# Recurrent attention issued between the MLP matmuls of earlier tokens, with its state kept in PSUM

## The chip, the cores and the metric

The kernel runs on one core of one Trainium2 chip. The metric is the time of one execution on the device in microseconds (us); the median of several executions is quoted. The span of a profile is a little shorter, since it runs from the first to the last instruction. PE is TensorE (matmuls), PEld its weight loads, DVE is VectorE, ACT ScalarE, POOL GpSimd, SP the engine whose queue issues the DMAs ("SPq" in the profile).

## The reference, cut to what matters

Decaying linear attention in blocks, and then an MLP on its output. There are 4 batches, 8 heads of 64, 768 tokens: 3072 tokens of 512 values. The MLP is 512 to 2048 to 512.

```python
for b in range(nb):                                  # attention, per batch and head
    intra = ((qb @ kb.T) * Dmask) @ vb               # within the block, causal, decay lam
    inter = (qb * lam_pow) @ kv_state                # from all earlier blocks
    out[block] = intra + inter
    kv_state = lam_block * kv_state + (kb * rev_pow).T @ vb
h = x @ w_in                                         # MLP on x = out, [3072, 512]
s = sin(alpha * h)
y = (h + s * s / (alpha + 1e-9)) @ w_out
```

Both kernels scale q by lam^i and k by lam^-i, so that the decay leaves the recurrence: the state becomes a plain sum over blocks. A "step" is one block of 128 tokens of one batch; a batch has 6 steps, the whole has 24. The MLP works on "chunks" of 512 tokens, that is four steps; there are 6 chunks.

## The kernel before

Two stages follow each other. First 24 steps of attention, each fed by three loads of 256 KB (q, k, v in pieces of 256 bytes):

```python
for s in range(NSTEP):                               # 24 steps
    gp.tensor_tensor(q2[js], q32[jd], Lq_b, ALU.mult)        # POOL: scale q, then k
    gp.tensor_tensor(k2[js], k32[jd], Lk_b, ALU.mult)
    ac.copy(v2[js], v32[jd])
    if s + 1 < NSTEP:
        emit_transposes(s + 1)                       # PE: 8 transposes; DVE: 2 copies to qT, kT
    for jp in range(4):                              # S = k q^T: 16 matmuls of 64x64, 128 columns
        for e in range(2):
            for kh in range(2):
                pe.matmul(S_ps[64*kh:64*kh+64, ...], kT[j][64*e:64*e+64, jp, ...], qT[j][...])
    if n <= NB - 2:                                  # Z = k^T v, 8 matmuls into PSUM
        ...                                          # cut
    ve.tensor_tensor(S_m[:, 0:512], S_ps[:, 0:512], mask, ALU.mult)      # two halves
    ve.tensor_tensor(S_m[:, 512:1024], S_ps[:, 512:1024], mask, ALU.mult)
    if n <= NB - 2:                                  # the state is kept in SBUF, in fp32
        ve.tensor_tensor(Zf, Zf, Z_ps[:, 0:256], ALU.add)
        ac.copy(Zs[s % 2], Zf)
    if n >= 1:                                       # state times q, 8 matmuls of 64x64
        pe.matmul(obank[64*e:64*e+64, jp, :], zsp[64*e:64*e+64, ...], qT[j][...])
    ...                                              # cut: 8 matmuls v^T S, two ACT copies to xT
    ...                                              # cut: casts of w1, w2; loads of step s + 3
```

Then the MLP, whose second layer follows one chunk behind the first:

```python
def h_group(idx, c, m):                              # 16 groups per chunk
    for kc in range(NKC):                            # 4 matmuls of 512 columns
        pe.matmul(hp[jh], w1[:, kc, 128*m:128*(m+1)], xT[:, kc, TCH*c:TCH*(c+1)])
    ac.activation(t16[jr], hp[jh], ACTF.Sin, scale=alpha_sb[:, m:m+1])
    gp.tensor_tensor(u16[jr], t16[jr], t16[jr], ALU.mult)               # POOL: the square
    ve.scalar_tensor_tensor(out=gT[c % 2][:, m, :], in0=u16[jr], scalar=r_sb[:, m:m+1],
                            in1=hp[jh], op0=ALU.mult, op1=ALU.add)
...                                                  # cut: waits on semaphores
phase_a(0)                                           # first layer, 64 matmuls
for c in range(1, NCH):
    phase_a(c)
    phase_b(c - 1)                                   # second layer, 64 matmuls
phase_b(NCH - 1)
```

Of the kernel before, what the change touches and what calls it, by code (L numbers as in the profile page):

```python
# [1 line left out]

# [3 lines left out]
ALU = mybir.AluOpType  # L7
# [7 lines left out]
class _Cnt:  # L15

    def __init__(self, h):
        self.h = h
        self.n = 0

    def add(self, k=1):
        self.n += k
        return self.n


def bass_lightning_attn__then__act_snake_kernel(
# [14 lines left out]
    NTOK = B * S  # L41
# [6 lines left out]
    NCH = NTOK // TCH  # L48
    NHP = 6
    TR = 6  # L50

    EV = [0, 2, 4, 6]
    OD = [1, 3, 5, 7]

    sp = nc.sync
    ac = nc.scalar
    pe = nc.tensor
    ve = nc.vector
    gp = nc.gpsimd

    es0 = contextlib.ExitStack()
    with es0:

        def sb(es, name, shape, dt):
            return es.enter_context(nc.sbuf_tensor(name, shape, dt))

        def pst(es, name, shape, dt=F32):
            return es.enter_context(nc.psum_tensor(name, shape, dt))

        def sem(name):  # L70
            return _Cnt(es0.enter_context(nc.semaphore(name)))

        xT = sb(es0, "xT", [128, 4, NTOK], BF16)
        w1 = sb(es0, "w1", [128, NKC, DFF], BF16)
        w2 = sb(es0, "w2", [128, NM, DM], BF16)
        w1s = sb(es0, "w1s", [128, NKC, DFF], F32)
        w2s = sb(es0, "w2s", [128, NM, DM], F32)
        alpha_sb = sb(es0, "alpha_sb", [128, NM], F32)

        c_dq = [sem(f"c_dq_{i}") for i in range(4)]  # L80
        c_dk = [sem(f"c_dk_{i}") for i in range(4)]
        c_dv = [sem(f"c_dv_{i}") for i in range(4)]
        c_q2, c_k2, c_v2 = sem("c_q2"), sem("c_k2"), sem("c_v2")
        c_tr = sem("c_tr")
        c_tev = sem("c_tev")
        c_S1E, c_S1O = sem("c_S1E"), sem("c_S1O")
        c_mE, c_mO = sem("c_mE"), sem("c_mO")
        c_2E, c_2O = sem("c_2E"), sem("c_2O")
        c_Z, c_Zf, c_Zs, c_Oev = sem("c_Z"), sem("c_Zf"), sem("c_Zs"), sem("c_Oev")
        c_lam, c_alpha = sem("c_lam"), sem("c_alpha")  # L90
        c_aT, c_asb = sem("c_aT"), sem("c_asb")
        c_gp, c_mask, c_Ef, c_id = sem("c_gp"), sem("c_mask"), sem("c_Ef"), sem("c_id")
        c_ln, c_lnL, c_L = sem("c_ln"), sem("c_lnL"), sem("c_L")
        c_r = sem("c_r")
        c_w1c, c_w2c = sem("c_w1c"), sem("c_w2c")
        c_w1d = [sem(f"c_w1d_{i}") for i in range(NKC)]
        c_w2d = [sem(f"c_w2d_{i}") for i in range(NM)]
        c_h, c_t, c_u, c_g = sem("c_h"), sem("c_t"), sem("c_u"), sem("c_g")
        c_o, c_oe = sem("c_o"), sem("c_oe")
        c_od = [sem(f"c_od_{i}") for i in range(2)]  # L100

        blk = es0.enter_context(nc.Block())

        @blk.sync
        def _(_unused_eng):
            esA = contextlib.ExitStack()
            esA.__enter__()
            RING = 3
            DRING = 4
            q32 = [sb(esA, f"q32_{i}", [128, H, D], F32) for i in range(DRING)]  # L110
            k32 = [sb(esA, f"k32_{i}", [128, H, D], F32) for i in range(DRING)]
            v32 = [sb(esA, f"v32_{i}", [128, H, D], F32) for i in range(DRING)]
            q2 = [sb(esA, f"q2_{i}", [128, H, D], BF16) for i in range(RING)]
            k2 = [sb(esA, f"k2_{i}", [128, H, D], BF16) for i in range(RING)]
            v2 = [sb(esA, f"v2_{i}", [128, H, D], BF16) for i in range(RING)]
            qT = [sb(esA, f"qT_{i}", [128, 4, 128], BF16) for i in range(2)]
            kT = [sb(esA, f"kT_{i}", [128, 4, 128], BF16) for i in range(2)]
            S_m = sb(esA, "S_m", [128, 8 * 128], BF16)
            mask = sb(esA, "mask", [128, 4, 128], BF16)
            maskf = sb(esA, "maskf", [128, 4, 128], F32)  # L120
            ident = sb(esA, "ident", [128, 128], BF16)
            identf = sb(esA, "identf", [128, 128], F32)
            Zf = sb(esA, "Zf", [128, 256], F32)
            Zs = [sb(esA, f"Zs_{i}", [128, 256], BF16) for i in range(2)]
            lam_bc = sb(esA, "lam_bc", [128, H], F32)
            lnlam = sb(esA, "lnlam", [128, H], F32)
            E_i = sb(esA, "E_i", [128, NB, H], I32)
            E_f = sb(esA, "E_f", [128, NB, H], F32)
            lnL = sb(esA, "lnL", [128, NB, H], F32)
            Lq = sb(esA, "Lq", [128, NB, H], F32)  # L130
            Lk = sb(esA, "Lk", [128, NB, H], F32)
            alphaT_sb = sb(esA, "alphaT_sb", [NM, 128], F32)
            ident16 = sb(esA, "ident16", [NM, NM], F32)
            S_ps = pst(esA, "S_ps", [128, 8 * 128])
            OE_ps = pst(esA, "OE_ps", [128, 4, 128])
            OO_ps = pst(esA, "OO_ps", [128, 4, 128])
            Z_ps = pst(esA, "Z_ps", [128, 256])
            T_ps = [pst(esA, f"T_ps_{i}", [128, 8, 128], BF16) for i in range(2)]

            def cb(h):  # L140
                return 4 * (h % 2) + h // 2

            sp.dma_start(
                lam_bc[:, :], bass.AP(lam.tensor, 0, [[0, 128], [1, H]])
            ).then_inc(c_lam.h, 16)
            c_lam.add(16)
            sp.dma_start(
                alphaT_sb[:, :],
                bass.AP(moe_alpha.tensor, 0, [[128, NM], [1, 128]]),
            ).then_inc(c_alpha.h, 16)  # L150
            c_alpha.add(16)

            def issue_step_loads(s):
                b = s // NB
                n = s % NB
                js = s % 4
                sl = slice(n * BL, (n + 1) * BL)
                src_q = q[b, :, sl, :].rearrange("h p d -> p h d")
                src_k = k[b, :, sl, :].rearrange("h p d -> p h d")
                src_v = v[b, :, sl, :].rearrange("h p d -> p h d")  # L160
                sp.dma_start(q32[js][:, :, :], src_q).then_inc(c_dq[js].h, 16)  # L161
                c_dq[js].add(16)
                sp.dma_start(k32[js][:, :, :], src_k).then_inc(c_dk[js].h, 16)  # L163
                c_dk[js].add(16)
                sp.dma_start(v32[js][:, :, :], src_v).then_inc(c_dv[js].h, 16)  # L165
                c_dv[js].add(16)

            issue_step_loads(0)
            issue_step_loads(1)
            issue_step_loads(2)  # L170

            gp.iota(
                E_i[:, :, :], [[128, NB], [0, H]], base=0, channel_multiplier=1
            ).then_inc(c_gp.h, 1)
            c_gp.add()
            gp.wait_ge(c_gp.h, c_gp.n)
            gp.tensor_copy(E_f[:, :, :], E_i[:, :, :]).then_inc(c_Ef.h, 1)
            c_Ef.add()
            gp.memset(maskf[:, :, :], 1.0).then_inc(c_gp.h, 1)
            c_gp.add()  # L180
            gp.wait_ge(c_gp.h, c_gp.n)
            gp.affine_select(
                out=maskf[:, :, :],
                in_=maskf[:, :, :],
                pattern=[[0, 4], [1, 128]],
                compare_op=ALU.is_ge,
                fill=0.0,
                base=0,
                channel_multiplier=-1,
            ).then_inc(c_gp.h, 1)  # L190
            c_gp.add()
            gp.wait_ge(c_gp.h, c_gp.n)
            gp.tensor_copy(mask[:, :, :], maskf[:, :, :]).then_inc(
                c_mask.h, 1
            )
            c_mask.add()
            gp.memset(ident16[:, :], 0.0).then_inc(c_gp.h, 1)
            c_gp.add()
            gp.wait_ge(c_gp.h, c_gp.n)
            gp.affine_select(  # L200
                out=ident16[:, :],
                in_=ident16[:, :],
                pattern=[[-1, NM]],
                compare_op=ALU.not_equal,
                fill=1.0,
                base=0,
                channel_multiplier=1,
            ).then_inc(c_gp.h, 1)
            c_gp.add()
            gp.memset(identf[:, :], 0.0).then_inc(c_gp.h, 1)  # L210
            c_gp.add()
            gp.wait_ge(c_gp.h, c_gp.n)
            gp.affine_select(
                out=identf[:, :],
                in_=identf[:, :],
                pattern=[[-1, 128]],
                compare_op=ALU.not_equal,
# [424 lines left out]
```

## Time and profile before

| | before |
|---|---|
| time, median of the four runs beside the change | 300.74 us |
| span of the profile | 299.0 us |
| attention, until the first MLP matmul | 126.0 us |
| MLP | 173 us |
| PE busy | 84% |

These are lines of the page of the kernel before: PE's busy time; the busy tenths of PE in 40 slices of 7.5 us; the granted PE clock in tenths; the busy tenths of the DMA engines and their GB/s; and the chain of work that ended last.

```profile
PE 251.4 (84%) x1841; PEld 135.2 (45%) x1857; DVE 143.9 (48%) x236; ACT 135.0 (45%) x218; POOL 150.7 (50%) x158
...
PE   0585447696778678699999999999999999999995
...
PEclk9999999999999999999999999999999999999999
DMA  7999999999999996000000100110011001000221
GB/s 145 217 273 268 277 286 210 233 219 246 243 226 243 247 204 137 2 0 0 0 3 35 70 37 1 64 76 3 0 70 70 2 36 70 37 0 35 95 83 70
...
PE 63%; SPq 23%; issue 5%; DMA 3%; ACT 2%; DVE 1%; POOL 1%; DVEq 0%; POOLq 0%; ACTq 0%
```

The two rows of DMA drop to nothing where PE goes to nine tenths, at slice 17. So the first stage is bound by DMA (and by the queue that issues it, the 23% of "SPq" in the chain) and leaves PE idle for a third of the time, and the second is bound by PE and leaves DMA nearly idle. Neither stage needs what the other has in plenty. The 84% of PE is an average over the two.

The windows of the same trace say it in us: length, then busy time and instructions of PE, PEld, DVE, ACT and POOL, the granted clock, DMA's share and GB/s.

```profile
80.00:100.00 20.00, 14.66 (x190) 10.75 (x188) 15.35 (x26) 10.17 (x19) 10.08 (x9) 1.00 1.13 236
...
216.50:238.00 21.50, 21.45 (x98) 9.78 (x100) 7.33 (x11) 10.55 (x16) 9.87 (x11) 1.00 0.13 50
```

One more thing is to be read from the attention stage, the pace of its small matmuls. In the timeline (start, length, what, how often) the second four transposes start 0.38 us after the first four:

```profile
86.45 0.58 PE L275 MATMUL T_ps<-ident,q_1 128*128 128x128 bf16 x4 [1.54 <-issue]
86.83 0.63 PE L280 MATMUL T_ps<-ident,k_1 128*128 128x128 bf16 x4
87.39 0.64 PE L338 MATMUL S_ps<-qT,kT 64*64 64x128 bf16 x16
```

That is 95 ns apart for 128 columns. In a later step the state's matmuls start at 119.70, 119.81, 119.91 and 120.02 us, about 107 ns apart. The MLP's matmuls of 512 columns take about 216 ns (64 of them from 157.56 to 171.37), so 128 columns should need some 55. The array runs at about half its rate here, although the row PEclk shows the full clock.

### The profile page before, as it was taken

How to read it: one execution, taken by the hardware profiler on the slowest of the kernel's cores; microseconds unless marked ns; L12 is line 12 of the kernel's file. 1: busy time of each engine (PE TensorE's matmuls, PEld its weight loads, DVE VectorE, ACT ScalarE, POOL GpSimd, SP SyncE). 2: the span in 40 equal slices, each digit the busy share in tenths (PEclk: the TensorE clock that was granted, in tenths of full speed). 3: DMA queues.
4: the chain of work that ended last, by engine and by line, in shares of the span. 5: the costliest groups of instructions: out<-in, count | busy, mean ns of one | idle time of the engine just before them, and what ended most of it. 6: DMA issues, size and time to landing. Idle time of an engine off the chain costs nothing.

```text
span 299.0 us, 5053 instructions
## 1 busy us (share of the span) xinstructions
PE 251.4 (84%) x1841; PEld 135.2 (45%) x1857; DVE 143.9 (48%) x236; ACT 135.0 (45%) x218; POOL 150.7 (50%) x158
## 2 busy tenths in 40 slices
PE   0585447696778678699999999999999999999995
PEld 0463335565556455434334444444444444444442
DVE  0463345486777866637775057307702760474000
ACT  4054322534535345477762277138515731771111
POOL 6523342544543644069996089319904970794000
PEclk9999999999999999999999999999999999999999
DMA  7999999999999996000000100110011001000221
GB/s 145 217 273 268 277 286 210 233 219 246 243 226 243 247 204 137 2 0 0 0 3 35 70 37 1 64 76 3 0 70 70 2 36 70 37 0 35 95 83 70
DMA packets 81416, 33.89 MB, mean 113 GB/s; under 512 B 75744, under 2 KB 75760, under 8 KB 80880
## 3 DMA queue, kind: packets, MB, share of 16 engines
q1 hardware_dynamic: 81392, 33.57, 47.5%
q8 instruction: 15, 0.25, 0.4%
q14 instruction: 9, 0.07, 0.1%
HBM read 27.28 MB, written 6.29 MB: 112 GB/s over the span
## 4 chain that ended last, share of the span: by engine, by line
PE 63%; SPq 23%; issue 5%; DMA 3%; ACT 2%; DVE 1%; POOL 1%; DVEq 0%; POOLq 0%; ACTq 0%
PE hp L527 29%; PE op L581 28%; SPq L165 11%; SPq L163 5%; DMA q_0<-in_q_dram 3%; SPq L161 3%; SPq L488 3%; PE S_ps L338 1%; SPq L482 1%; PE T_ps L275 1%; PE OE_ps L429 1%; PE OE_ps L417 1%; PE OO_ps L442 1%; PE T_ps L280 1%; ACT xT L455 1%
## 5 line engine op out<-in xcount | busy, mean ns | idle before, releaser
L527 PE MATMUL hp<-xT,w 128*128 128x512 bf16 x375 | 87.1, 388 | 2.3 <-ACT xT L455 1.8
L581 PE MATMUL op<-w,gT 128*128 128x512 bf16 x377 | 83.3, 379 | 0.4
L527 PEld LDWEIGHTS hp<-xT,w 128*128 128x128 bf16 x384 | 37.2, 100 | 51.3 <-DVE gT L557 5.5
L581 PEld LDWEIGHTS op<-w,gT 128*128 128x128 bf16 x384 | 37.6, 98 | 45.3
L593 ACT COPY osb<-op 128x512 f32<-128x512 f32 x24 | 14.0, 585 | 68.3 <-PE op L581 68.3
L289 DVE COPY qT<-T_ps 128x512 bf16<-128x512 bf16 x24 | 10.2, 424 | 47.9 <-PE T_ps L280 47.9
L405 ACT CAST Zs<-Zf 128x256 bf16<-128x256 f32 x20 | 8.1, 405 | 54.2 <-DVE Zf L400 38.2
L549 POOL TENSOR_TENSOR u_0<-t_0 128x512 bf16<-128x512 bf16 x16 | 16.6, 1037 | 23.7 <-ACT t_0 L539 23.7
L549 POOL TENSOR_TENSOR u_2<-t_2 128x512 bf16<-128x512 bf16 x16 | 16.6, 1038 | 23.0 <-ACT t_2 L539 23.0
L557 DVE SCALAR_TENSOR_TENSOR gT<-u_2,r_sb,hp 128x512 bf16<-128x512 bf16 x16 | 12.0, 748 | 27.2 <-POOL u_2 L549 27.2
L549 POOL TENSOR_TENSOR u_4<-t_4 128x512 bf16<-128x512 bf16 x16 | 16.6, 1038 | 11.6 <-ACT t_4 L539 11.6
L557 DVE SCALAR_TENSOR_TENSOR gT<-u_0,r_sb,hp 128x512 bf16<-128x512 bf16 x16 | 12.0, 748 | 20.1 <-POOL u_0 L549 20.1
L557 DVE SCALAR_TENSOR_TENSOR gT<-u_4,r_sb,hp 128x512 bf16<-128x512 bf16 x16 | 12.0, 748 | 15.7 <-POOL u_4 L549 15.7
L454 ACT CAST xT<-OE_ps 64x512 bf16<-64x512 f32 x24 | 13.9, 578 | 11.9 <-PE OO_ps L442 11.4
L373 DVE TENSOR_TENSOR S_m<-S_ps,mask 128x512 bf16<-128x512 f32 x24 | 16.6, 691 | 0.8 <-issue 0.8
L549 POOL TENSOR_TENSOR u_3<-t_3 128x512 bf16<-128x512 bf16 x16 | 16.6, 1037 | 0.1
L549 POOL TENSOR_TENSOR u_1<-t_1 128x512 bf16<-128x512 bf16 x16 | 16.6, 1037 | 0.0
L549 POOL TENSOR_TENSOR u_5<-t_5 128x512 bf16<-128x512 bf16 x16 | 16.6, 1037 | 0.0
L383 DVE TENSOR_TENSOR S_m<-S_ps,mask 128x512 bf16<-128x512 f32 x24 | 16.4, 681 | 0.0
L275 PE MATMUL T_ps<-ident,q_1 128*128 128x128 bf16 x32 | 4.7, 301 | 13.3 <-issue 10.7
L338 PE MATMUL S_ps<-qT,kT 64*64 64x128 bf16 x384 | 15.4, 311 | 0.0
L455 ACT CAST xT<-OO_ps 64x512 bf16<-64x512 f32 x24 | 13.9, 580 | 0.3
(110 smaller groups left out, 372.6 us busy)
## 6 DMA issues: line engine op xcount, KB each, us to landing
out_dram<-osb SPq DMA_DIRECT2D x24, 256.0 KB, 2.0
w1s<-in_moe_w_in_dram SPq DMA_DIRECT2D x4, 1024.0 KB, 6.7
w2s<-in_moe_w_out_dram SPq DMA_DIRECT2D x16, 256.0 KB, 4.7
q_0<-in_q_dram SPq DMA_DIRECT2D x6, 256.0 KB, 4.9
k_0<-in_k_dram SPq DMA_DIRECT2D x6, 256.0 KB, 5.9
v_0<-in_v_dram SPq DMA_DIRECT2D x6, 256.0 KB, 5.1
q_1<-in_q_dram SPq DMA_DIRECT2D x6, 256.0 KB, 5.2
k_1<-in_k_dram SPq DMA_DIRECT2D x6, 256.0 KB, 5.6
```

The costliest lines, as they stand in the source:

```text
L163: sp.dma_start(k32[js][:, :, :], src_k).then_inc(c_dk[js].h, 16)
L165: sp.dma_start(v32[js][:, :, :], src_v).then_inc(c_dv[js].h, 16)
L338: ins = pe.matmul(S_ps[64 * kh:64 * kh + 64, 128 * cb(h):128 * (cb(h) + 1)], kT[j][64 * e:64 * e + 64, jp, 64 * kh:64 * kh + 64], qT[j][64 ...
L373: ve.tensor_tensor(S_m[:, 0:512].rearrange("p (c i) -> p c i", i=128), S_ps[:, 0:512].rearrange("p (c i) -> p c i", i=128), mask[:, :, :], ...
L383: ve.tensor_tensor(S_m[:, 512:1024].rearrange("p (c i) -> p c i", i=128), S_ps[:, 512:1024].rearrange("p (c i) -> p c i", i=128), mask[:, ...
L454: ac.copy(xT[0:64, :, tok0:tok0 + BL], OE_ps[0:64, :, :])
L455: ac.copy(xT[64:128, :, tok0:tok0 + BL], OO_ps[64:128, :, :]).then_inc(c_Oev.h, 1)
L527: last = pe.matmul(hp[jh][:, :], w1[:, kc, 128 * m:128 * (m + 1)], xT[:, kc, TCH * c:TCH * (c + 1)], start=(kc == 0), stop=(kc == NKC - 1),)
L549: gp.tensor_tensor(u16[jr][:, :], t16[jr][:, :], t16[jr][:, :], ALU.mult).then_inc(c_u.h, 1)
L557: ve.scalar_tensor_tensor(out=gT[c % 2][:, m, :], in0=u16[jr][:, :], scalar=r_sb[:, m:m + 1], in1=hp[jh][:, :], op0=ALU.mult, op1=ALU.add, ...
L581: last = pe.matmul(opsm[jo][:, :], gT[c % 2][:, m, 128 * s4:128 * (s4 + 1)], w2[:, m, :], start=(m == 0), stop=(m == NM - 1),)
L593: ac.copy(osb[jo][:, :], opsm[jo][:, :]).then_inc(c_oe.h, 1)
```

## The change

The intent is to fill each stage's idle resource with the other's work. Only four steps of attention run before the MLP. The next four run after chunk 0. The steps of chunk c + 1 are then issued between the first-layer matmuls of chunk c: S after every second group of four, the rest of the step two groups later. PE's operations stay in the order in which they are written down ("as recorded" in the diff below), so the order is the design.

Three smaller parts come with it. The state stays in PSUM (the matmuls of k^T v accumulate over a batch; ACT copies it to SBUF each step). It is applied as four block-diagonal 128x128 matmuls, two heads each, instead of eight of 64x64, and S takes 8 matmuls instead of 16, so that a step has 36 PE operations instead of 48. And a small recorder takes operations with their reads, writes and an assumed duration, sorts those of every engine but PE by a greedy simulation (the earliest that can start; among these the one recorded first), and puts in the semaphores.

The core of the diff, with cuts marked:

```diff
+    def schedule(self, hop=0.12, rate=270e3, dma_fixed=2.0, issue=0.65):
...
+                if e == "PE":
+                    ...                                     # PE: as recorded
+                else:
+                    t0 = min(max(free[e], ready_at[o]) for o in pend[e])
+                    op = min((o for o in pend[e] if max(free[e], ready_at[o]) <= t0 + 1e-9),
+                             key=lambda o: (o.prio, o.idx))
...
+        def w2_block(j):
+            i = j % 2                                       # two staging tiles for four blocks
+            src = moe_w_out[512 * j:512 * (j + 1), :].rearrange("(m p) d -> p m d", p=128)
+            rec("SP", lambda e: e.dma_start(w2s[i][:, :, :], src), 0, writes=[f"w2s.{i}"],
+                slot=f"w2s{i}", nbytes=1 << 20)
+            rec("DVE", lambda e: e.tensor_copy(w2[:, 4 * j:4 * (j + 1), :], w2s[i][:, :, :]), 1.2, ...)
+        def prep(s):                                        # POOL: scale q, then k; ACT: copy v
...
+        def att_T(s, bank=None):                            # 8 transposes, one DVE copy
+            rec("PE", pe, 0.75, reads=[f"q2.{c}", f"k2.{c}", "ident"], writes=[key])
...
+        def att_S(s):                                       # 8 matmuls of 64 rows x 128, one DVE mask
+            rec("PE", pe, 0.6, reads=[f"qkT.{j}"], writes=["S0", "S1"])
...
+        def att_O(s, bank=None):
+                if has_state:
+                    for jp in range(HP):                    # block-diagonal: two heads at once
+                        e.matmul(dst[:, jp, :], Zs[(s - 1) % 2][:, jp, :], qkT[j][:, jp, :],
+                                 start=(jp == 0), stop=False, skip_group_check=True)
...
+                            last = e.matmul(                # the state accumulates in PSUM
+                                Z_ps[64 * h:64 * h + 64, jp, :], k2[c][:, 2 * jp + h, :], v2[c][...],
+                                start=(n == 0 and jp == 0), stop=(n == NB - 2 and jp == HP - 1), ...)
...
+        load(0); consts(); ...                              # steps 0 to 3, w1
+        load(4)
+        load(5)
+        for j in range(4):
+            w2_block(j)
+        for s in range(6, 9):
+            load(s)
+        for m in range(NM):
+            grp_A(0, m)                                     # first layer of chunk 0
...
+        for m4 in range(4):
+            for s4 in range(4):
+                grp_B(0, s4, m4, banks[s4])                 # second layer of chunk 0
+        prep_next(4)
+        att_T(4)
+        for s in range(4, 8):                               # steps 4 to 7, alone
+            prep_next(s + 1)
+            att_S(s)
+            att_O(s)
+            att_T(s + 1)
...
+        for c in range(1, NCH):
+            base = 4 * (c + 1)
+            for m in range(NM):
+                grp_A(c, m)
+                if base < NSTEP and m % 2 == 1:             # steps 8 to 23, in between
+                    s = base + m // 4
+                    if m % 4 == 1:
+                        att_S(s)
+                    else:
+                        att_O(s)
+                        if s + 1 < NSTEP:
+                            if s == base + 3:
+                                prep_next(s + 1)
+                            att_T(s + 1)
+            for s4 in range(4):
+                bank = next_bank()
+                for m4 in range(4):
+                    grp_B(c, s4, m4, bank)
+                ...                                         # prep_next of the steps to come
```

## The prediction

> **What bounds it now.** The span is 299.0 us in two stages. Until 125 us attention runs and PE is no limit: the chain of waits is mostly issues on the load queue, and DMA moves 210 to 286 GB/s (slice table) until all 24 step loads and 8.4 MB of weights are in. From 126 us the MLP is PE-bound: busy 98 to 99% (windows), 49 matmuls of 512 columns in 10.74 us, 219 ns each, so 768 need 168 us. Attention matmuls of 128 columns follow each other at about 105 ns (four transposes in 0.38 us), not the 55 ns that 219 would scale to. The Trainium skill, "TensorE: Matmul & The Clock Gate", Part 1, gives 106.7 ns for a cold array and 55.6 warm; the trace agrees with cold.
>
> **What changes.** Only steps 0 to 3 precede the MLP; 4 to 7 run alone after chunk 0; 8 to 23 sit between matmuls of chunks 1 to 4. A step's matmuls fall from 48 to 36. The DMA-bound 125 us should shrink to the DMA that chunk 0 needs, and the PE work of 16 steps is added to the MLP's 168 us.
>
> **Sum** (estimates from durations in the trace).
> 1. To the end of chunk 0: a step load takes 3.5 us (three issues of 1.15 us in the timeline), a megabyte of weights 3.2. The first layer starts near 26 us (four loads, alpha, first w1 block, 1.6 us cast); 16 groups follow at POOL's 1.04 us square. The last two w2 blocks wait for a staging buffer, and I read the recorder to put loads 6 to 11 ahead of the last: 12 loads, 8.4 MB, alpha: landed at 73 us, second layer done at 78. PE idles some 15 us there.
> 2. Steps 4 to 7, serial: S 0.7, mask 1.3 (two 0.69 halves now), O and Z 1.4, transposes 1.0, copy 0.8, hops: 5.3 each, 22: 100.
> 3. Chunks 1 to 4: 28.0 us of MLP each, four steps at 2.2 us warm PE (36 pitches of 55 to 60 ns, switches of tile mode), 1.5 us stalls: 38 each, 153: 253. POOL (25), ACT (21) and DVE (21) fit; in the first layer DVE is near 86%.
> 4. Chunk 5 has no attention: POOL's 16.6 us paces it, the second layer waits for its last square: 31, then 3 us copy and output: 286 span, time about 1.5 over it as in before.
>
> So it gains 13 us: serial steps 4 to 7, the wait for w2, and attention on PE eat most of what the overlap hides.
>
> **Predicted** 286 us, 8 in 10 between 267 and 300. Faster by over 2%: 0.74; within 2%: 0.18; slower: 0.08.
>
> **What would show it.** Step 1: PE nearly idle to 26 us and again between 50 and 70, its wait naming w2's cast or DMA; DMA above 230 GB/s until 70. Step 2: 20 us with PE half idle; mask, copy, PE alternate. Step 3: PE above 93% busy, 37 to 39.5 us a chunk, 128-column matmuls at 56 to 70 ns. Step 4: squares back to back in the last first layer.
>
> **What would make it wrong.** Loads issued after w2's blocks: 12 us better. 128-column matmuls staying at 105 ns, or a stall on mask, copy or bank at each insertion: 1.5 us times 16, up to 25 us worse. Engine orders fixed by wrong modelled durations, so that an engine sits at a wait for late data: unbounded.

## The result, and the profile after

| | before | after |
|---|---|---|
| time, median | 300.74 us | 271.73 us |
| range of the four runs | 299.39 to 300.93 | 270.51 to 272.61 |
| span | 299.0 us | 270.4 us |
| PE busy | 251.4 us, 84% | 222.9 us, 82% |

The ratio is 0.906, with a 95% interval of 0.902 to 0.910. A ratio is the mean time of one kernel's runs over that of the other's in the same rounds, so it is not quite the ratio of the medians. The change is faster by 9.4%, inside the predicted range and better than its middle by 14 us.

The same lines of the page after:

```profile
PE 222.9 (82%) x1584; PEld 108.9 (40%) x1584; DVE 123.9 (46%) x159; ACT 120.7 (45%) x214; POOL 148.9 (55%) x151
...
PE   0346998822954699899999899999999999999895
...
PEclk9995599995795579999999999999999999999999
DMA  8999999999999965655230012100121001210022
GB/s 164 220 209 393 240 292 269 205 238 335 209 219 283 229 153 119 156 119 155 78 80 0 2 39 78 41 1 2 40 78 41 0 2 39 78 41 0 0 78 78
...
PE 49%; POOL 18%; DVE 11%; DMA 7%; ACT 5%; SPq 5%; issue 4%; POOLq 1%; ACTq 0%
```

PE now starts on the MLP in slice 5, and DMA goes on to slice 21 beside it (a slice is 6.8 us here). PE is busy for 28 us less in all. In e4 below, which has the same operations without the overlap, it is busy for 66.4 us before the first MLP matmul, against 82.5 in the kernel before, so some 16 us of the 28 come with the fewer operations. The rest fits the faster pace of the small matmuls between those of the MLP. But the row of PE has two holes, in slices 9 and 10 and in slices 12 to 14, and the chain names POOL for 18%, against 1% before. The waits of PE show what the first hole is (who waited for whom, total us, times, longest):

```profile
PE m_ps L458 <- DVE w L343: 12.8, 3, 10.2
...
PE A_ps L382 <- DVE qkT L373: 6.6, 10, 0.9
PE A_ps L401 <- DVE S_m L386: 4.3, 4, 1.3
```

The second layer of chunk 0 (line 458) waits 10.2 us in one piece for the cast of the third block of w2, and the chain of waits shows that the cast waits for DMA; its columns are start, length, what. The transfer of that block, from its issue on, is the row at 56.90:

```profile
55.95 0.91 SPq L290
56.90 8.05 DMA w2s<-in_moe_w_out_dram
64.97 1.24 DVE w L343
66.25 9.17 PE m_ps L458 x32
75.91 0.70 DVE qkT L373
...
77.10 1.24 DVE S_m L386
```

The block is issued late because 14 loads of later steps stand before it in SP's order (all of steps 6 to 9 and two v of steps 10 and 11, by the timeline). The staging tile that it reuses was free long before: the cast of the first block ended at 47.35 us (45.96, 1.39 long). After the second layer ends, the last two rows begin the second hole: steps 4 to 7, in which DVE's copy and mask alternate with PE.

Within the interleaved chunks a step now costs PE this (timeline of chunk 1: the second half of step 8 and the transposes of step 9; the last row is the next MLP group):

```profile
99.83 0.39 PE L401 MATMUL A_ps<-qkT,Zs 128*128 128x128 bf16 x4
100.15 0.41 PE L405 MATMUL A_ps<-S_m,v_3 128*64 128x128 bf16 x8
100.40 0.29 PE L420 MATMUL Z_ps<-v_3,k_3 128*64 128x64 bf16 x8
100.62 0.40 PE L368 MATMUL A_ps<-ident,q_4 128*128 128x128 bf16 x4
100.85 0.39 PE L370 MATMUL A_ps<-ident,k_4 128*128 128x128 bf16 x4
101.08 0.38 PE L441 MATMUL m_ps<-xT,w 128*128 128x512 bf16 x1
```

From start to start: state 0.32 us, output 0.25, new state 0.22, eight transposes 0.46, that is 58 ns each. With 0.34 us for S (97.75 to 98.09 in the same timeline) a step takes 1.59 us of PE. The transposes that stood 95 ns apart now stand 58 apart. The Trainium skill, "TensorE: Matmul & The Clock Gate", Part 1, gives 55.6 ns warm and 106.7 cold for 128 columns; both paces are nearly met in these two traces (58 and about 107).

The timeline of POOL in the same chunk shows where its 18% come from (u are the squares of the first layer; k and q are the scalings for later steps):

```profile
101.93 1.04 POOL L352 TENSOR_TENSOR k_3<-k_1,Lk 128x512 bf16<-128x512 f32 x1
102.93 1.04 POOL L350 TENSOR_TENSOR q_4<-q_2,Lq 128x512 bf16<-128x512 f32 x1
103.93 1.04 POOL L447 TENSOR_TENSOR u_0<-t_0 128x512 bf16<-128x512 bf16 x1
104.93 1.04 POOL L447 TENSOR_TENSOR u_1<-t_1 128x512 bf16<-128x512 bf16 x1
105.93 1.04 POOL L447 TENSOR_TENSOR u_2<-t_2 128x512 bf16<-128x512 bf16 x1
106.93 1.04 POOL L447 TENSOR_TENSOR u_3<-t_3 128x512 bf16<-128x512 bf16 x1
107.92 1.04 POOL L352 TENSOR_TENSOR k_4<-k_2,Lk 128x512 bf16<-128x512 f32 x1
```

No gap is left: six operations of 1.0 us for every four groups, 6.0 us, while PE needs 4 times 0.865 and one step of 1.59, 5.05 us. In this stretch POOL sets the pace, although over the whole chunk it is busy for less time than PE.

By stage, from the starts of the layers in the timeline:

| stage | predicted, us | measured, us |
|---|---|---|
| to the end of chunk 0 | 78 | 75.3 |
| steps 4 to 7 | 22 | 18.9 (75.3 to 94.2) |
| chunks 1 to 4 | 153 | 143.0 (94.2 to 237.2) |
| chunk 5 | 31 | 30.1 (to 267.3) |
| last copy and output | 3 | 3.1 (to 270.4) |

### The profile page after: what moved, and what is told of

Its sections match the earlier page's. It is cut to its first block, busy times and chain, and to the rows that moved or that the text cites. A ratio compares the mean times of both kernels' runs of the same rounds, so it can differ in the third digit from the quotient of the medians.

```text
span 270.4 us, 4030 instructions
## 1 busy us (share of the span) xinstructions
PE 222.9 (82%) x1584; PEld 108.9 (40%) x1584; DVE 123.9 (46%) x159; ACT 120.7 (45%) x214; POOL 148.9 (55%) x151
## 4 chain that ended last, share of the span: by engine, by line
PE 49%; POOL 18%; DVE 11%; DMA 7%; ACT 5%; SPq 5%; issue 4%; POOLq 1%; ACTq 0%
PE m_ps L458 25%; PE m_ps L441 15%; POOL u_2 L447 5%; SPq L290 4%; POOL u_1 L447 4%; DVE gT L449 4%; POOL u_0 L447 3%; POOL u_3 L447 3%; DVE S_m L386 3%; DMA w2s<-in_moe_w_out_dram 3%; PE A_ps L382 3%; DVE qkT L373 2%; DMA v_3<-in_v_dram 2%; DMA v_2<-in_v_dram 2%; PE A_ps L405 1%
## 5 line engine op out<-in xcount | busy, mean ns | idle before, releaser
L458 PE MATMUL m_ps<-w,gT 128*128 128x512 bf16 x384 | 87.1, 386 | 14.8 <-DVE w L343 12.8
L441 PE MATMUL m_ps<-xT,w 128*128 128x512 bf16 x384 | 94.4, 392 | 0.8 <-ACT xT L414 0.5
L458 PEld LDWEIGHTS m_ps<-w,gT 128*128 128x128 bf16 x384 | 37.1, 99 | 63.1 <-DVE w L343 14.2
L441 PEld LDWEIGHTS m_ps<-xT,w 128*128 128x128 bf16 x384 | 35.5, 100 | 46.5 <-DVE gT L449 6.9
L386 DVE TENSOR_TENSOR S_m<-A_ps,mask 128x1024 bf16<-128x1024 f32 x24 | 29.4, 1224 | 53.0 <-PE A_ps L382 52.9
L466 ACT COPY osb<-m_ps 128x512 f32<-128x512 f32 x24 | 14.1, 586 | 79.2 <-PE m_ps L458 77.4
L449 DVE SCALAR_TENSOR_TENSOR gT<-u_0,r_sb,m_ps 128x512 bf16<-128x512 bf16 x24 | 17.9, 744 | 24.3 <-POOL u_0 L447 24.2
L445 ACT ACTIVATE t_2<-m_ps,alpha_sb 128x512 bf16<-128x512 f32 x24 | 16.5, 687 | 15.0 <-PE m_ps L441 15.0
L449 DVE SCALAR_TENSOR_TENSOR gT<-u_2,r_sb,m_ps 128x512 bf16<-128x512 bf16 x24 | 17.9, 747 | 6.3 <-POOL u_2 L447 6.3
L449 DVE SCALAR_TENSOR_TENSOR gT<-u_1,r_sb,m_ps 128x512 bf16<-128x512 bf16 x24 | 17.9, 746 | 4.9 <-POOL u_1 L447 4.9
L373 DVE COPY qkT<-A_ps 128x1024 bf16<-128x1024 bf16 x20 | 13.7, 686 | 13.9 <-PE A_ps L370 13.9
L445 ACT ACTIVATE t_0<-m_ps,alpha_sb 128x512 bf16<-128x512 f32 x24 | 16.5, 687 | 6.0 <-PE m_ps L441 5.8
L449 DVE SCALAR_TENSOR_TENSOR gT<-u_3,r_sb,m_ps 128x512 bf16<-128x512 bf16 x24 | 17.8, 742 | 2.3 <-POOL u_3 L447 2.3
L445 ACT ACTIVATE t_1<-m_ps,alpha_sb 128x512 bf16<-128x512 f32 x24 | 16.5, 687 | 4.8 <-PE m_ps L441 4.7
L445 ACT ACTIVATE t_3<-m_ps,alpha_sb 128x512 bf16<-128x512 f32 x24 | 16.5, 687 | 4.8 <-PE m_ps L441 4.5
L428 ACT CAST Zs<-Z_ps 64x256 bf16<-64x256 f32 x40 | 14.7, 367 | 0.5
```

Of the source, the lines that this page charges most:

```text
L373: rec("DVE", lambda e: e.tensor_copy(qkT[j][:, :, :], dst), 0.7, reads=[key], writes=[f"qkT.{j}"])
L386: rec("DVE", lambda e: e.tensor_tensor(S_m[j][:, :, :], A_ps[:, :, :], mask_b, ALU.mult), 1.25, reads=["S0", "S1", "mask"], writes=[f"S_m. ...
L428: rec("ACT", lambda e, rows=rows, cols=cols: e.copy(Zs[j][rows, :, cols], Z_ps[rows, :, :]), 0.4, reads=["Z"], writes=[f"Zs.{j}"])
L441: last = e.matmul(m_ps[i][:, :], w1[:, kc, 128 * m:128 * (m + 1)], xT[x][:, kc, :], start=(kc == 0), stop=(kc == NKC - 1))
L445: rec("ACT", lambda e: e.activation(t16[tt][:, :], m_ps[i][:, :], ACTF.Sin, scale=alpha_sb[:, m:m + 1]), 0.7, reads=[f"m.{i}", "alpha"], w ...
L449: rec("DVE", lambda e: e.scalar_tensor_tensor(out=gT[g][:, m, :], in0=u16[tt][:, :], scalar=r_sb[:, m:m + 1], in1=m_ps[i][:, :], op0=ALU.m ...
```

## The experiments

Twelve kernels were run, all with correct results. A ratio is to the kernel before in the same rounds; 0.01 is 3.0 us. "Changed" is the kernel after the change.

| run | time, median us | ratio to before, 95% interval |
|---|---|---|
| changed | 271.73 | 0.906 (0.902 to 0.910) |
| e1_w2_early | 259.54 | 0.865 (0.859 to 0.870) |
| e2_prep_in_B | 267.39 | 0.892 (0.887 to 0.897) |
| e3_fill_wait | 261.94 | 0.874 (0.869 to 0.879) |
| e4_attn_first | 310.53 | 1.035 (1.028 to 1.041) |
| e5_twice_T | 273.50 | 0.913 (0.909 to 0.917) |
| e6_twice_T_prep_in_B | 271.68 | 0.909 (0.904 to 0.914) |
| e7_state_by_head | 271.70 | 0.908 (0.904 to 0.912) |
| e9_durations | 268.36 | 0.896 (0.891 to 0.899) |
| e8_w2_prep | 254.31 | 0.847 (0.842 to 0.852) |
| e10_steps_in_B0 | 255.05 | 0.849 (0.843 to 0.855) |
| e11_last_chunk | 252.85 | 0.841 (0.836 to 0.846) |
| e12_room_out | 242.11 | 0.808 (0.805 to 0.811) |

The first four ask where the gain comes from and what the three visible losses cost.

### e4_attn_first: the overlap alone undone

```diff
-    NX = 3
-    RL = 6
+    NX = 6                                  # x of all chunks is kept
+    RL = 5                                  # room
...
+        for s in range(NSTEP):              # all 24 steps first
+            prep(s + 1); att_S(s); att_T(s + 1, ...); att_O(s, ...)
+            ...                             # w1 after steps 0 to 3, w2 after 6, 9, 12, 15
+        for c in range(NCH):                # then chunk by chunk
+            ...                             # 16 grp_A, then 16 grp_B
```

> The interleaving alone undone: all 24 steps first, in the same recorder with the same operations, PSUM state and block-diagonal state; then six chunks of MLP (load ring of 5 instead of 6, six x tiles instead of 3, for room). Mine (the gain is the overlap; the cheaper steps are worth nothing while DMA bounds them): attention takes 110 to 125 us, the MLP 175 to 180 since each first layer without attention is paced by POOL, together 290 to 306 us, that is within 3% of the kernel before. Rival (the fewer matmuls, the state in PSUM or the recorder's fewer semaphores bring a good part): below 285 us.

It took 310.53 us, slower than the kernel before. The first MLP matmul stands in the timeline at

```profile
124.59 0.64 PE L405 MATMUL m_ps<-S_m,v 128*64 128x128 bf16 x8
125.16 2.31 PE L441 MATMUL m_ps<-xT,w 128*128 128x512 bf16 x5
```

against 126.0 us before. So with 36 PE operations a step instead of 48, single copies and masks, and the state in PSUM, attention alone is only 1 us shorter while DMA bounds it (POOL waits 56.5 us in all for loads of q). The MLP is slower than before, at 29.9 us a chunk (in the chain of waits the long parts of the second layers start at 145.40, 175.30, 205.20, 235.10 and 265.00), since here the second layer follows its own first layer at once and waits for the last square; before, it followed one chunk behind. The expectation of 290 to 306 was missed by 4 us on the high side. In the same recorder with the same operations, overlapping is worth 310.5 - 271.7 = 39 us. About 11 of these are e4's slower MLP (184.2 us, to the end of its span, against 173), which comes of the order of its layers; without them, overlapping is worth about 28 us, which is the whole gain of 29 within 1 us.

### e1_w2_early: weights before loads that nobody needs yet

```diff
-            rec("SP", lambda e: e.dma_start(w2s[i][:, :, :], src), 0, writes=[f"w2s.{i}"], ...)
+            st, key = (w2s[i], f"w2s.{i}") if j < 2 else (w1s[i], f"w1s.{i}")   # a free w1 tile
+            rec("SP", lambda e: e.dma_start(st[:, :, :], src), 0, writes=[key], ...)
...
+            if j == 1:                      # loads of step 6 and later are recorded to wait
+                held.append(op)             # for the cast of w1's second block
```

> The last two w2 blocks are staged in free w1 tiles and issued before the loads of steps 6 and later, instead of behind loads 6 to 11. Mine (the 10.2 us idle of PE before the second half of chunk 0's second layer is data queued behind 4.7 MB of loads that nobody needs yet): that idle goes, chunk 0 ends near 63 us instead of 75.4, the time falls by 9 to 12 us, to about 261. Rival (steps 4 to 7 need loads 6 to 8 anyway, so the wait only moves behind chunk 0): chunk 0 ends earlier but the attention steps then wait for loads 6 to 8, and the time falls by less than 4 us.

It took 259.54 us, 12 us less. In the timeline the second layer of chunk 0 waits 1.26 us at its start and once more inside, for the casts of the first two blocks, and then runs through:

```profile
46.25 3.71 PE L463 MATMUL m_ps<-w,gT 128*128 128x512 bf16 x16 [1.26 <-DVE w L348]
51.23 10.53 PE L463 MATMUL m_ps<-w,gT 128*128 128x512 bf16 x48 [1.26 <-DVE w L348]
```

It ends at 61.6 us instead of 75.3. Steps 4 to 7 then take 20.0 us (61.6 to 81.6) instead of 18.9. This is not a wait for the loads of steps 6 to 8: PE's waits there are as long as in the changed kernel (1.3 to 1.4 us at a mask, 0.8 to 0.9 at a copy). The slow pace came sooner: the state matmuls of step 4 take 0.53 us from start to start instead of 0.33, and from 64.7 us on the granted clock is 0.50, while after the change step 4 and the transposes behind it still ran at full pace. My theory held and the rival fell: the wait was the order of the queue, not the amount of data. The edit changes the staging tile and the order together. That the order is what counted is read from the trace above, where the old tile was free 9.5 us before the issue.

### e3_fill_wait: work put into the wait

```diff
         for m4 in range(4):
+            if m4 == 2:                     # before the third w2 block
+                prep_next(4)
+                att_T(4)
+                for s in range(4, 6):
+                    ...                     # prep_next, att_S, att_O, att_T as below
             for s4 in range(4):
                 grp_B(0, s4, m4, banks[s4])
-        for s in range(4, 8):
+        for s in range(6, 8):
```

> Steps 4 and 5 are put into PE's wait for the third w2 block, the order of DMA up to there stays. Mine (that wait is DMA's, and PE has nothing to do in it): the two steps cost nothing there, 8 us of the 17.2 of the serial steps go, the time is about 263.5. Rival (the steps' own loads, scalings or copies are late too, or DVE's casts and the steps' masks get into each other's way): less than 4 us.

It took 261.94 us, 9.8 us less, somewhat more than the 8 expected, and the rival fell. Two of the serial steps cost nothing when they stand in the hole, and PE's wait for w2 shrinks to 2.06 us at that place:

```profile
64.55 0.61 PE L368 MATMUL A_ps<-ident,q 128*128 128x128 bf16 x4
64.95 0.63 PE L370 MATMUL A_ps<-ident,k 128*128 128x128 bf16 x4
67.64 9.61 PE L458 MATMUL m_ps<-w,gT 128*128 128x512 bf16 x32 [2.06 <-DVE w L343]
```

### e2_prep_in_B: the scalings moved off the first layer

```diff
+            sq = rec("POOL", ...)           # the square in grp_A is handed back
...
     def prep(s): ...
-        rec("POOL", ..., writes=[f"q2.{c}"])
+        rec("POOL", ..., writes=[f"q2.{c}"], after=gate)      # k alike
...
+            gate[:] = [sq]                  # after the first layer of each chunk from 1 on
             for s4 in range(4):
                 bank = next_bank()
```

> The scalings of q and k on POOL for steps 13 and later are held back until the last square of a first layer, so that they run under the second layer, where POOL is idle. Nothing else changes. Mine (chunks 1 to 3 are paced by POOL, 24 operations of 1.0 us in the first layer): the first layers fall from 28.2, 24.7 and 23.9 us to 20 to 22 each, near chunk 4's 19.9, and the time falls by 11 to 16 us, to about 258. Rival (the first layers are paced by DVE at 80 to 85% and by the waits for mask, copy and bank at each inserted step): the first layers stay above 23 us and the time falls by less than 3 us.

It took 267.39 us, 4.3 us less, where I had expected 11 to 16. The mechanism was right and my expectation of its size was a misreading: I had taken windows that end where a wait ends, 2.75 us into the second layer, for the first layers of chunks 1 to 3, but not for chunk 4, and so compared unlike pieces. Measured from the first matmul of one layer to the first of the next, the first layers were 23.4, 21.9, 21.3 and 20.0 us in the changed kernel (94.19 to 117.59, 132.03 to 153.90, 168.12 to 189.37, 203.46 to 223.41), and are 22.4, 20.3, 20.2 and 20.0 us here. Chunks 1 to 4 together fell from 143.0 to 138.1 us. In the chain of waits of this run chunk 3 is PE alone (the rows cut are PE's attention work):

```profile
179.08 1.73 PE m_ps L443 x8
...
181.14 1.83 PE m_ps L443 x8
...
184.21 13.81 PE m_ps L461 x64
198.03 1.73 PE m_ps L443 x8
```

So POOL's order cost 5.0 us, and the rival (DVE, or the waits at each insertion) is not what paced these chunks. What is left of chunk 1, 2 us over its neighbours, contains the restart after the serial steps: its first eight matmuls take 3.6 us, where eight take 1.9 later.

### e5_twice_T and e6_twice_T_prep_in_B: PE work doubled where it may or may not count

```diff
-            c, j = s % RC, s % 2
+            c, j, twice = s % RC, s % 2, 2 if s > 8 else 1
...
-                for jp in range(HP):        # both loops of transposes
+                for jp in list(range(HP)) * twice:
```

e6 has the edit of e2_prep_in_B in addition.

> The changed kernel with each transpose of steps 9 to 23 done twice into the same place (same result): 8 more PE operations a step, 0.46 us at the 58 ns pitch that the trace shows, 15 times 0.46 = 6.9 us of PE work. Mine (chunks 1, 2 and 3 are paced by POOL and have about 1.7, 2.0 and 1.3 us of PE slack each, as the run with the scalings held back showed; chunk 4 has none): about 5 us of it are absorbed, the time rises by 2 to 3.5 us, to about 274.5. Rival (PE is the limit all through the interleaved chunks): it rises by the full 7 us, to 278.5.

> The same doubled transposes on the kernel with the scalings held back for the second layer (267.4 us). Mine (there PE is the limit of chunks 1 to 4): it rises by the full 6 to 7.5 us, to about 274, so that both doubled kernels end up equal. Rival (something else than PE or POOL paces the chunks, DVE for instance): it rises by less than 4 us.

On the changed kernel 15 times 0.46 = 6.9 us more of PE work cost 1.8 us by the medians. By chunk (first layer to first layer) the lengths went from 37.8, 36.1, 35.3, 33.8 to 37.7, 36.1, 35.8, 35.1: chunks 1 and 2 absorb all of it, chunk 4 nothing. On the kernel with the scalings held back they went from 36.2, 34.1, 34.0, 33.8 to 36.4, 35.9, 35.8, 35.1: chunks 2 to 4 pay in full, 1.8 us for four steps and 1.3 for three. The total is 4.3 us by the medians and 5.2 by the ratios, below my 6 to 7.5, because chunk 1 paid only 0.2; there the full pace came sooner in that run (its first eight matmuls took 2.2 us until the next S, where e2's took 3.6). The two doubled kernels ended 1.8 us apart, nearly equal as expected. The 4.3 us alone would hardly separate my theory from the rival's "less than 4"; the chunks do. So PE work in the interleaved chunks is free where POOL is slower, and is paid in full where it is not.

### e9_durations: only the recorder's assumptions changed

```diff
-            rec("PE", pe, 0.75, ...)        # transposes        +  0.46
-            rec("PE", pe, 0.6, ...)         # S                 +  0.34
-            rec("PE", pe, 0.9, ...)         # state and output  +  0.57
-                rec("PE", pz, 0.3, ...)     # new state         +  0.22
```

> Only the durations that the recorder assumes for the attention work on PE are changed, to the warm ones of the trace (0.46, 0.34, 0.57, 0.22 us instead of 0.75, 0.6, 0.9, 0.3); the emitted work is the same, and the order on POOL has about half as many scalings inside the first layers of chunks 1 to 3. Mine (the assumed slowness of PE made the recorder fill POOL gaps that do not exist): 1.5 to 3.5 us faster, about 269. Rival (a greedy order puts some scalings into the first layers whatever the durations, and a few are enough to pace them): less than 1 us.

It took 268.36 us, 3.4 us less, the upper end of the expectation, with no operation added or removed; only the order on the engines other than PE differs. Chunks 1 to 4 took 137.8 us, as in e2_prep_in_B, although only 7 of 17 scalings left the squares' part of chunks 1 to 3: three, four and three stand between the squares there, where the changed kernel has six, six and five. The recorder had been told that a step costs PE 2.55 us, when it costs 1.59. The likely reason is that with 2.55 its simulated POOL had gaps in the first layers, which the greedy rule filled. The second layers had room: POOL is busy there for 4.4, 4.2 and 1.8 of about 14 us in the changed kernel.

### e7_state_by_head: the block-diagonal application undone

```diff
-                        e.matmul(dst[:, jp, :], Zs[(s - 1) % 2][:, jp, :], qkT[j][:, jp, :], ...)
+                        for h in range(2):
+                            rows, cols = slice(64 * h, 64 * h + 64), slice(64 * h, 64 * h + 64)
+                            e.matmul(dst[rows, jp, :], Zs[(s - 1) % 2][rows, jp, cols],
+                                     qkT[j][rows, jp, :], ...)
```

> The block-diagonal application alone undone: eight 64x64 matmuls a step for the state instead of four 128x128, in the changed kernel. Mine (pairs of 64x64 matmuls run side by side, as before the change, so that eight cost what four do, plus a switch of tile mode of about 0.1 us, 20 times): the time stays within 2 us, at 270 to 274. Rival (the halved count matters): four more pitches of 58 ns and switches, 0.4 us or more a step, 5 to 8 us slower.

It took 271.70 us; the ratios, 0.908 and 0.906, have overlapping intervals, and chunks 1 to 4 take 143.2 us against 143.0. So four block-diagonal matmuls are worth nothing measurable against eight of 64x64. This fits the Trainium skill, "TensorEngine Tiling (Array Packing)", Key Properties, which says that different tiles can load and multiply in parallel; here eight cost nearly what four do. But in chunks 1 to 3 POOL would hide a small cost on PE, so only chunk 4 speaks directly: 34.25 us instead of 33.78 for four steps, 0.12 us a step.

### e8_w2_prep: both repairs

The edits of e1_w2_early and e2_prep_in_B together.

> The two repairs together: w2 blocks issued before the loads of steps 6 and later, and the scalings held back for the second layers. Mine: the two costs lie one after the other, so the gains add, 12 + 4.3 = 16 us, about 255.5. Rival (with chunk 0 over 14 us earlier, the loads of later steps, now behind w2, are late for the interleaved steps): gains add to less than 13 us.

It took 254.31 us, 17.4 us less than the changed kernel. The two gains add (12.2 and 4.3; the 0.9 us over their sum are within the noise), as they lie one after the other.

### e10_steps_in_B0: the serial steps moved into chunk 0's second layer

```diff
         for m4 in range(4):
             for s4 in range(4):
                 grp_B(0, s4, m4, banks[s4])
+                if m4 == 0 and s4 == 0:
+                    att_T(4)
+                if s4 == 1:
+                    prep_next(5 + m4)
+                    att_S(4 + m4)
+                if s4 == 3:
+                    att_O(4 + m4)
+                    att_T(5 + m4)
-        ...                                 # steps 4 to 7 behind it
```

> On top of both repairs, steps 4 to 7 go between the matmuls of chunk 0's second layer instead of behind it. Mine (the serial steps cost 4.6 us each for about 1.6 us of warm PE work, the rest is PE waiting for mask and copy): 18.8 us become 6 to 7 plus up to 4 us of waiting for loads 6 to 8, so 8 to 12 us faster than without, about 245.5. Rival (the loads of steps 6 to 8 land too late, DMA bounds it): less than 5 us.

It took 255.05 us, no faster than without (254.31). The steps did move: chunk 1 started at 74.48 us instead of 81.86. What was gained was given back at once in two new waits of PE, here in the table of waits:

```profile
PE m_ps L448 <- ACT osb L474: 7.2, 1, 7.2
PE A_ps L375 <- POOL k L359: 4.8, 1, 4.8
```

The rival that I had named (loads of steps 6 to 8 too late) is not what it was. The 7.2 us are in the timeline: chunk 0's first three output copies run from 70.5 us, the fourth only at 86.32, and PE's fifth group of chunk 1 needs the bank that this copy reads:

```profile
72.49 0.60 ACT L474 COPY osb<-m_ps 128x512 f32<-128x512 f32 x1
...
81.97 1.13 SPq L477 DMA_DIRECT2D out_dram<-osb  x1
...
86.32 0.59 ACT L474 COPY osb<-m_ps 128x512 f32<-128x512 f32 x1 [5.41 <-DMA out_dram<-osb]
...
86.96 3.60 PE L448 MATMUL m_ps<-xT,w 128*128 128x512 bf16 x8 [7.17 <-ACT osb L474]
```

There are three output tiles. The fourth copy waits for the first output transfer to land, which is issued at 81.97, although its data was ready at 71.1, because loads stand before it in the fixed order of SP's queue. The 4.8 us are the first transposes of step 4, put so early that POOL was still at chunk 0's squares.

### e11_last_chunk: the last two second layers

On top of e10, the groups of chunk 5's first layer alternate with those of chunk 4's second layer (in the loop over m: a grp_B of chunk 4 before each grp_A of chunk 5).

> On top of that, the groups of the last first layer alternate with those of chunk 4's second layer. Mine (the last first layer takes 18.5 us for 13.8 us of PE work since POOL's 16 squares pace it and the second layer waits for the last of them): 4 to 5 us faster than without, about 241. Rival (five PSUM banks or ACT's copies of outputs stop the alternation): less than 2 us.

It took 252.85 us, 2.2 us less, where I had expected 4 to 5. The expectation rested on the same misreading as e2's: the last first layer takes 14.7 us (237.24 to 251.93 in the changed kernel), not 18.5; only 0.9 us of it and a wait of 1.2 us behind it could be had, and that is what came.

### e12_room_out: the new waits removed

```diff
-    NO = 3
+    NO = 4                                  # a fourth output tile
...
+        # order in chunk 0's second layer: T of step 4 after group 4, S after 6, 9, 12, 15,
+        # the rest of a step after 8, 11, 14 and at the end
```

> On the last kernel, two changes to the new stalls that its predecessor's trace shows: a fourth output tile, since PE waited 7.2 us for the fourth output copy of chunk 0, which waited for the first output transfer, which stood behind 11 us of loads on the queue; and the first transposes of step 4 four groups later, since PE waited 4.8 us there for POOL to finish chunk 0's squares. Mine (these two stalls swallowed what moving steps 4 to 7 gained): 8 to 11 us faster than 252.9, about 243. Rival (DMA bounds the first 85 us whatever PE does, another wait takes their place): less than 4 us.

It took 242.11 us, 10.7 us less, as expected; both waits are gone from PE's table, but the two changes were not run apart. Steps 4 to 7 and chunk 0's second layer together end at 71.4 us, 22.8 us earlier than in the changed kernel. This version is faster than both kernels: 0.808 of the kernel before (0.805 to 0.811), 10.9% under the changed one by the medians. Its row of PE has no hole after the start:

```profile
PE 211.3 (88%) x1556; PEld 105.8 (44%) x1584; DVE 124.1 (52%) x159; ACT 119.8 (50%) x214; POOL 151.8 (63%) x151
...
PE   0256599779979889999999999999999999999994
```

What is left is mainly the first 28.8 us, in which four steps and the first weights are loaded, and the 166 us that 768 matmuls take at 216 ns.

## Why the prediction was right, point by point

**What bounds the kernel before.** Right. The stage of attention is DMA's: shortening everything else in it (e4) moved its end from 126.0 to 125.2 us.

**Step 1, to the end of chunk 0: 78 us predicted, 75.3 measured.** Right in size and in cause. The first layer started at 28.5 us (26 predicted). The wait for w2 was predicted as 15 us of idle PE and came as 1.3 before each of the first two blocks and 10.2 before the third. The prediction gave two grounds for it, a staging buffer and loads put ahead. The buffer was free at 47.35 us, so it was the loads, and e1's 12.2 us match the "12 us better" that the prediction gave for loads issued after w2's blocks.

**Step 2, the serial steps: 22 us predicted, 18.9 measured.** Right in kind: mask, copy and PE alternate in the chain. They went faster in part because DVE's fused operations are shorter than I took them (mask 1.22 us, copy 0.69 us, together 0.2 us a step) and because the array was still warm in the first of them.

**Step 3, chunks 1 to 4: 153 us predicted, 143.0 measured.** This is the term that was mis-sized, and it makes most of the 14 us. The prediction said "four steps at 2.2 us warm PE (36 pitches of 55 to 60 ns, switches of tile mode)". The pitch was right, but 2.2 us was not: a step takes 1.59 us, since the pairs of column-tiled matmuls run side by side (eight output matmuls in 0.25 us) and a switch of mode costs about 0.1 us (four state matmuls took 0.32 us, four pitches of 58 ns are 0.23). Counted with the parts that steps lack at the end of a batch or of the work, attention takes some 24 us of these chunks, not 35. The MLP is 27.7 us a chunk and not 28.0: the "49 matmuls in 10.74 us" of the trace before were about one too few, as its record holds 375 and 377 of 384. With these two the sum would have been 141; the stalls, predicted as 6 us, were then about 8: 143.0 less 4 times 27.7 and 24.3 leaves 8.

**"POOL (25), ACT (21) and DVE (21) fit; in the first layer DVE is near 86%."** The totals fit, but I named the wrong engine. POOL paced the first layers of chunks 1 to 3 because the recorder put six, six and five scalings between their squares. e2 takes all of them out and e9 seven of the 17, by two different means, and both make chunks 1 to 4 shorter by 5 us; e5 shows that PE had slack in chunks 1 and 2, and e6 that in chunks 2 to 4 it has none once POOL is relieved. The cause that I listed as a risk, "engine orders fixed by wrong modelled durations", was real, and worth 3.4 us.

**Step 4: 31 and 3 us predicted, 30.1 and 3.1 measured.** Right: the 16 squares stand back to back from 239.07 to 255.1 us.

**"It gains 13 us".** It gained 29. The mechanism and the stages were right; about 10 us of the difference is step 3, and 6 us are steps 1 and 2.

What stays open: whether the half pace of the array in the serial steps is only the idle time of PE. In these traces it comes and goes with the gaps, but no run isolates it. The state in PSUM and the halved number of S matmuls were not run apart either: e4 shows that all the cheaper parts together gain 1 us while DMA bounds attention, but not what each saves between the MLP's matmuls.

## What to carry to other kernels

When one stage is bound by DMA and the next by the matmul engine, look first at what overlapping them would give, and cost the small matmuls at the pace that they have in a dense stream (here 58 ns instead of 95 to 107), not at the pace of the stage in which they idle. Then read each engine by the stretch in which it is needed and not over a whole period: POOL, busy for 60 to 67% of chunks 1 to 3, paced their first layers, because its deferrable work stood in the wrong half. And when waits are removed by reordering, follow every in-order queue to its next fixed order, since twice here the gain was held up by data queued behind loads that nobody needed yet.

## What the Trainium skill lacked or had wrong

- "TensorE: Matmul & The Clock Gate", Back-to-back issue gap, gives 131 ns per matmul for a sustained stream of weight loads and matmuls of 512 columns and 81 ns for 128 columns. Here 64 pairs of 512 columns took 13.81 us, 216 ns each, and transposes of 128 columns stood 58 ns apart, near the section's figures for the isolated gap instead.
- The same page, Part 4, says that the array does not reach its full clock for transposes and gives about 275 ns for one. Here four transposes amid the MLP's matmuls took 0.40 us from first start to last end, at a spacing of 58 ns. The trace lists them as MATMUL and does not show whether the transpose mode was on, and no run shows whether transposes alone would bring the full pace.
- The same page, Part 1, warns that the clock events in traces are unreliable on trn2. That agrees: the row of the granted clock is full throughout the attention stage before and in e4, where four transposes took 0.58 to 0.63 us. In the serial steps after, the record and the pace agree: 0.50 from 82 to 94 us, where they took 0.61 to 0.63. The spacing of equal matmuls is the better witness.
- "TensorEngine Tiling (Array Packing)", Key Properties, says that a change of tiling mode drains the engine, without a figure. Estimated from the timeline after it costs about 0.1 us in a warm stream, as above.
- No page that I found warns of an output left unissued because loads stand before it in the fixed order of the issuing queue: here (e10) a transfer whose data was ready at 71.1 us was issued at 81.97.
